# Attention's weighted sums transposed onto the two column halves of the array, two query tiles a step, gates from the unnormalised sums

## The chip, the cores and the metric

One Trainium2 chip, one of its cores. The metric is the device time of one execution in microseconds (us), the median of several runs. Lower is better.

## What is computed

Three blocks follow each other: attention over a band of keys and a few global ones, a layer of eight experts with one expert for each token, and a gated product.

```python
# attention: batch 2, 8 heads, 768 positions, head dimension 64; 8 global keys, 96 local ones
scores = q @ k.T / 8 + bias          # bias: -slope[head] * distance
scores = where(keep, scores, -1e9)   # keep: key among the first 8, or 0 <= query - key < 96
a = exp(scores - max(scores)); a = a / (sum(a) + 1e-9)
x = a @ v                            # gathered to (1536 tokens, 512)

# experts: 8 of them, 512 -> 1024 -> 512
logits = x @ w_gate; e = argmax(logits)
gate = softmax(logits)[e]; eom = sigmoid(x @ w_output_gate)[e]
y = gate * eom * (relu(x @ w1[e]) @ w2[e])

# gated product, width 1536
out = ((y @ w_a) * (y @ w_b)) @ w_out
```

## The kernel before

The kernel runs the blocks one after the other; the change is in attention and its names reach a little into the routing that follows.

**Attention** goes over 48 units (batch, pair of heads, query tile of 128). For one unit, 256 key columns are laid out side by side: 96 keys of the tile ahead, 32 global columns, the tile's own 128 (the first tile of a head has its own 128 alone). A unit has three parts, written for different units in one turn of the loop, so that the engines overlap: in turn n the loop writes `score` of unit n, `trans` of unit n-2 and `av` of unit n-3.

- `score`: the two heads of a pair sit in the two halves of the partitions (64 rows each), so their matmuls use the two row halves of TensorE's array. VectorE adds the bias and takes the row's extreme in one instruction (L489), ScalarE takes the exponential (L493).
- `trans`: the weights `pe` (queries in the partitions) are transposed by TensorE in chunks of 128 keys (L505), and copied out of PSUM as `pt` (keys in the partitions), two times in three by ScalarE (L509), else by VectorE (L511).
- `av`: `pt` is the stationary operand and the values `vc`, 64 columns and a 65th of ones, the moving one (L523, L526). The result `ps_a` has queries in the partitions, and its 65th column is the sum of the weights. Every second unit VectorE adds 1e-9 (L530), takes the reciprocal (L531) and multiplies into `x` (L535).

**Gates.** `gate` transposes a finished piece of `x` back (L548, `ps_xt`), ScalarE copies it as `xT` (L550), and TensorE multiplies it by the two gates' 16 columns (L555, `ps_g`); VectorE adds the four pairs of heads up in `lg` (L558, L560). A queue `gq` holds these steps, one a turn.

**Routing** sorts tokens by expert. `r_expert` finds each token's expert, `r_rank` its place (a few small matmuls into `ps_r`), `r_hot` and `r_ids` make the list of tokens. For the first batch these come from a queue `eq`, one entry a turn of the attention loop; for the second they follow the loop. `eload` and `esplit` fetch and split the first expert's weights in the last turns: a cast on ScalarE (L103) and a subtraction on GpSimd (L104).

All float32 products of attention are two matmul instructions each in the trace (transposes one). The order on each engine is the order of the code; engines meet by semaphores. PSUM holds two score buffers, two for `trans` (shared with `ps_xt`), one for `ps_a` and one for `ps_g`.

Of the kernel before, what the change touches and what calls it, by code (L numbers as in the profile page):

```python
# [46 lines left out]
def moe_block_kernel(ctx, tc, qd, kd, vd, kt, vn, nv, wg, we, wm, out):  # L47
# [19 lines left out]
    wg_sb = con([P, 4, 16], "wg_sb")  # L67
    lg = con([P, NT, 16], "lg")
# [324 lines left out]
    with ExitStack() as att:  # L393
# [33 lines left out]
        nc.sync.dma_start(wg_sb, wg)  # L427
        make_identity(nc, ident)
# [39 lines left out]
        units = [(b, p, i) for b in range(B) for p in range(4) for i in range(QT)]  # L468
        PE_, PT, pA = {}, {}, {}
# [4 lines left out]
        def score(u):  # L474
            b, p, i = u
            k0, n, b0 = geom(i)

            ps = psS.tile([P, 2, 512], F32, tag="s", name="ps_s")
            bp = b * 4 + p
            ko, qo = (0, 0) if bp or i < 2 else (K1, Q0)  # L480
            for j in range(2):
                r = slice(j * D, (j + 1) * D)
                T.matmul(ps[:, j, 0:n], QQ[bp, qo][r, i * P - qo:(i + 1) * P - qo], KC[bp, ko][r, k0 - ko:k0 - ko + n],
                         start=True, stop=True)
            pe = wrk.tile([P, 2, 256], F32, tag="pe", bufs=4, name="pe")
            mx = wrk.tile([P, 2], F32, tag="mx", bufs=6, name="mx")

            for j in range(2):
                V.tensor_tensor_reduce(  # L489
                    out=pe[:, j, 0:n], in0=ps[:, j, 0:n], in1=bias[2 * p + j][:, b0:b0 + n], op0=ALU.add, op1=ALU.min,  # L490
                    scale=-0.125, scalar=3e38, accum_out=mx[:, j:j + 1])
            for j in range(2):
                A.activation(pe[:, j, 0:n], pe[:, j, 0:n], AF.Exp, bias=mx[:, j:j + 1], scale=-1.0)  # L493
            PE_[u] = pe

        ncopy = [0]

        def trans(u):
            b, p, i = u
            pe = PE_.pop(u)  # L500
            nch = 1 if i == 0 else 2
            ps = psT.tile([P, 2, 2, P], F32, tag="t", name="ps_t")
            for j in range(2):
                for c in range(nch):
                    T.transpose(ps[:, j, c, :], pe[:, j, c * P:(c + 1) * P], ident)  # L505
            pt = wrk.tile([P, 2, 2, P], F32, tag="pt", name="pt")
            ncopy[0] += 1
            if ncopy[0] % 3 or u in units[-2:]:
                A.copy(pt[:, :, 0:nch, :], ps[:, :, 0:nch, :])  # L509
            else:  # L510
                V.tensor_copy(pt[:, :, 0:nch, :], ps[:, :, 0:nch, :])  # L511
            PT[u] = pt

        def av(u):
            b, p, i = u
            pt = PT.pop(u)
            if i % 2 == 0:
                pA[b, p] = psA.tile([P, 2, 2, 65], F32, tag="a", name="ps_a")
            pa = pA[b, p]
            for j in range(2):  # L520
                bh = b * H + 2 * p + j
                if i == 0:
                    T.matmul(pa[:, 0, j, :], pt[:, j, 0, :], VC[bh][:, 0, :], start=True, stop=True)  # L523
                else:
                    for c in range(2):
                        T.matmul(pa[:, i % 2, j, :], pt[:, j, c, :], VC[bh][:, 2 * i - 1 + c, :], start=(c == 0), stop=(c == 1))  # L526
            if i % 2 == 1:
                pa = pA.pop((b, p))
                rs = wrk.tile([P, 2, 2, 1], F32, tag="rs", bufs=4, name="rs")
                V.tensor_scalar(rs, pa[:, :, :, 64:65], 1e-9, None, ALU.add)  # L530
                V.reciprocal(rs, rs)  # L531
                m = b * 3 + i // 2
                if p == 0:
                    xt[m] = xp.tile([P, 2, DM], F32, tag="x", name=f"x{m}")
                V.tensor_tensor(  # L535
                    xt[m][:, :, 2 * p * D:(2 * p + 2) * D].rearrange("p i (j d) -> p i j d", j=2),
                    pa[:, :, :, 0:64], rs.to_broadcast([P, 2, 2, 64]), ALU.mult)
                if p == 3:
                    nc.sync.dma_start(x_dram[m * 256:(m + 1) * 256, 0:DM].rearrange("(i p) d -> p i d", p=P), xt[m])


        xTs = {}

        def gate(m, p, k):
            if k == 0:
                pt = psT.tile([P, 2, P], F32, tag="t", bufs=2, name="ps_xt")
                for j in range(2):
                    T.transpose(pt[:, j, :], xt[m][:, j, p * P:(p + 1) * P], ident)  # L548
                xTs[m, p] = wrk.tile([P, 2, P], F32, tag="xT", bufs=3, name="xT")
                A.copy(xTs[m, p], pt)  # L550
            else:
                xs = xTs.pop((m, p))
                pg = psG.tile([P, 2, 16], F32, tag="g", bufs=1, name="ps_g")
                for j in range(2):
                    T.matmul(pg[:, j, :], xs[:, j, :], wg_sb[:, p, :], start=True, stop=True)  # L555
                L = lg[:, 2 * m:2 * m + 2, :]
                if p == 0:
                    V.tensor_copy(L, pg)  # L558
                else:
                    V.tensor_tensor(L, pg, L, ALU.add)  # L560
# [4 lines left out]
        gq, eq = [], []  # L565
# [20 lines left out]
        for n in range(nu + 3):  # L586
            if n < nu:
                b, p, i = units[n]
                nxt = b * 4 + p + 1
                if i in (2, 3) and nxt + 1 < 8:  # L590
                    (loadq if i % 2 else loadk)(nxt + 1)
                if i in (4, 5) and nxt < 8:
                    loadv(2 * nxt + i - 4)
                if b == 0 and p < 3 and i in (3, 5):
                    make_bias(2 * p + 2 + (i - 3) // 2)
                score(units[n])
            if 0 <= n - 2 < nu:
                trans(units[n - 2])
            if 0 <= n - 3 < nu:
                av(units[n - 3])  # L600
            for q in (gq, eq):
                if q:
                    q.pop(0)()
            if 0 <= n - 3 < nu:
                b, p, i = units[n - 3]
                if i % 2 == 1:
                    m = b * 3 + i // 2
                    gq += [lambda k=k, m=m, p=p: gate(m, p, k) for k in range(2)]
                if n == 29:
                    route(0, 6)  # L610
                    factor(0, 6)
            for _ in range(2 if n >= 7 else 0):
                if cl:
                    cl.pop(0)()
            if n == 3:
                flags()
# [577 lines left out]
```

## Time and profile before

| | |
|---|---|
| median of 3 runs | 657.28 us (655.16 to 664.75) |
| the profiled execution | 651.98 us |
| its span, first to last instruction | 650.3 us |
| PE busy | 602.3 us, 93% |
| DVE / ACT / POOL busy | 401.7 / 310.2 / 215.7 us |
| granted clock of PE, mean | 0.971 |
| attention | from 4.5 us (first score matmul) to some 124 us (last gates) |

The span's share of an engine is an average over blocks of very different kind; attention is read in its own stretch. PE is TensorE's matmuls, PEld its weight loads, DVE VectorE, ACT ScalarE, POOL GpSimd. A matmul's end is modelled, and its shown duration reaches over the next one; where blocks of matmuls follow each other, the distance from start to start tells what a block takes.

### The profile page before, as it was taken

How to read it: one execution, taken by the hardware profiler on the slowest of the kernel's cores; microseconds unless marked ns; L12 is line 12 of the kernel's file. 1: busy time of each engine (PE TensorE's matmuls, PEld its weight loads, DVE VectorE, ACT ScalarE, POOL GpSimd, SP SyncE). 2: the span in 40 equal slices, each digit the busy share in tenths (PEclk: the TensorE clock that was granted, in tenths of full speed). 3: DMA queues.
4: the chain of work that ended last, by engine and by line, in shares of the span. 5: the costliest groups of instructions: out<-in, count | busy, mean ns of one | idle time of the engine just before them, and what ended most of it. 6: DMA issues, size and time to landing. Idle time of an engine off the chain costs nothing. (4 is left out here: it accounts for less than half of the span.)

```text
span 650.3 us, 9929 instructions
## 1 busy us (share of the span) xinstructions
PE 602.3 (93%) x3503; PEld 517.7 (80%) x3503; DVE 401.7 (62%) x936; ACT 310.2 (48%) x609; POOL 215.7 (33%) x167
## 2 busy tenths in 40 slices
PE   6999999667999999799788999999999999999995
PEld 4778778557999988689787888888888888888884
DVE  6566776559684798799996765754551675131312
ACT  3655557324554666577664656554521554111110
POOL 3000004135343655465354543363330354001012
PEclk9999999858999999799899999999999999999998
DMA  7454541435747777777635332232110130001011
GB/s 259 136 159 147 185 162 44 110 123 196 255 144 251 212 242 257 232 234 243 200 129 175 103 119 71 65 130 65 66 65 1 65 130 0 1 1 65 1 66 65
DMA packets 33357, 84.09 MB, mean 129 GB/s; under 512 B 5232, under 2 KB 11632, under 8 KB 33296
## 3 DMA queue, kind: packets, MB, share of 16 engines
q1 hardware_dynamic: 21200, 53.29, 25.9%
q10 hardware_dynamic: 9936, 23.14, 10.6%
q0 software_dynamic: 2160, 6.91, 2.9%
q8 instruction: 30, 0.49, 0.3%
q14 instruction: 31, 0.25, 0.1%
HBM read 72.23 MB, written 11.10 MB: 128 GB/s over the span
## 5 line engine op out<-in xcount | busy, mean ns | idle before, releaser
L104 POOL TENSOR_TENSOR wl<-st,wh 128x1024 fp32r<-128x1024 f32 x27 | 65.8, 2441 | 173.8 <-ACT wh L103 162.9
L1097 PE MATMUL ps_ab<-yTh,wh 128*128 128x512 f32 x288 | 112.7, 391 | 1.9 <-ACTq L996 1.9
L1098 PE MATMUL ps_ab<-yTl,wh 128*128 128x512 f32 x288 | 112.7, 391 | 0.0
L1099 PE MATMUL ps_ab<-yTh,wl 128*128 128x512 f32 x288 | 112.4, 390 | 0.0
L880 POOL TENSOR_TENSOR wl<-wl,st 128x512 fp32r<-128x512 f32 x36 | 56.4, 1568 | 141.7 <-ACT wl L879 132.3
L1106 DVE TENSOR_TENSOR a<-a,ps_ab 128x512 f32<-128x512 f32 x36 | 24.7, 686 | 112.5 <-PE ps_ab L1099 106.9
L103 ACT CAST wh<-st 128x1024 fp32r<-128x1024 f32 x64 | 67.2, 1052 | 13.4 <-DMA st<-we 12.0
L700 PE MATMUL ps_y<-h,wl 128*128 128x256 f32 (+5 forms) x256 | 70.5, 275 | 0.0
L700 PE MATMUL ps_h<-x,wl 128*128 128x256 f32 (+5 forms) x256 | 69.3, 271 | 0.0
L1097 PEld LDWEIGHTS ps_ab<-yTh,wh 128*128 128x128 f32 x288 | 54.0, 188 | 14.1 <-ACTq L996 2.1
L1104 ACT COPY a<-ps_ab 128x512 f32<-128x512 f32 x36 | 21.1, 585 | 90.8 <-PE ps_ab L1099 89.0
L493 ACT ACTIVATE pe<-pe,mx 128x256 f32<-128x256 f32 (+1 forms) x96 | 41.8, 483 | 47.4 <-DVE mx L489 47.1
L1099 PEld LDWEIGHTS ps_ab<-yTh,wl 128*128 128x128 f32 x288 | 54.0, 188 | 11.9
L1098 PEld LDWEIGHTS ps_ab<-yTl,wh 128*128 128x128 f32 x288 | 54.0, 188 | 11.7
L696 PE MATMUL ps_y<-h,wh 128*128 128x448 f32 (+3 forms) x160 | 54.3, 393 | 7.7 <-DVE h L714 7.1
L104 DVE TENSOR_TENSOR wl<-st,wh 128x1024 fp32r<-128x1024 f32 x37 | 52.4, 1419 | 10.2 <-ACT wh L103 10.2
L1107 ACT CAST gh<-a 128x512 fp32r<-128x512 f32 x36 | 22.3, 619 | 71.7 <-DVE a L1106 71.4
L1120 PE MATMUL ps_o<-wl,gh 128*128 128x512 f32 x144 | 56.3, 391 | 0.0
L1119 PE MATMUL ps_o<-wh,gh 128*128 128x512 f32 x144 | 56.2, 390 | 0.0
L1121 PE MATMUL ps_o<-wh,gl 128*128 128x512 f32 x144 | 56.2, 390 | 0.0
L881 POOL TENSOR_TENSOR wl<-wl,td 128x512 fp32r<-128x512 f32 x36 | 52.5, 1459 | 2.8
L700 PEld LDWEIGHTS ps_y<-h,wl 128*128 128x128 f32 x256 | 50.8, 198 | 0.0
(181 smaller groups left out, 1286.2 us busy)
## 6 DMA issues: line engine op xcount, KB each, us to landing
st<-we SPq DMA_DIRECT2D x63, 512.0 KB, 4.1
st<-wm ACTq DMA_DIRECT2D x36, 512.0 KB, 3.8
vc<-vd SPq DMA_DIRECT2D x16, 357.5 KB
k<-kd SPq DMA_DIRECT2D x7, 464.0 KB, 4.9
x_dram<-x SPq DMA_DIRECT2D x6, 512.0 KB, 2.9
st<-y_dram SPq DMA_DIRECT2D x6, 512.0 KB
q<-qd SPq DMA_DIRECT2D x7, 384.0 KB, 5.3
y_dram<-zero SPq DMA_DIRECT2D x4, 256.0 KB
```

The costliest lines, as they stand in the source:

```text
L103: A.copy(wh, st)
L104: eng.tensor_tensor(wl, st, wh[:, :].bitcast(F32), ALU.subtract)
L696: T.matmul(pt[:, 0:2 * n].rearrange("p (s n) -> p s n", s=2), a, M[:, k], start=(k == 0), stop=False)
L700: T.matmul(pt[:, 0:n], b, M[:, k, 0], start=False, stop=(k == last))
L880: G.tensor_tensor(wl_, wl_.bitcast(F32), sv[:, :, 0].bitcast(F32), ALU.add)
L881: G.tensor_tensor(wl_, wl_.bitcast(F32), td[:, :].bitcast(F32), ALU.mult)
L1097: T.matmul(pt, wh[:, s_, k, :], yh[:, k, :], start=(k == 0), stop=False)
L1098: T.matmul(pt, wh[:, s_, k, :], yl[:, k, :], start=False, stop=False)
L1099: T.matmul(pt, wl_[:, s_, k, :], yh[:, k, :], start=False, stop=(k == 3))
L1119: T.matmul(PO[c][t_], a, wh, start=(f == FG * g), stop=False)
L1120: T.matmul(PO[c][t_], a, wl_, start=False, stop=False)
L1121: T.matmul(PO[c][t_], l, wh, start=False, stop=(f == FG * g + FG - 1))
```

## The change

A step now holds two query tiles: 24 units (batch, pair of heads, pair of tiles), with `trans` one step behind `score`, `av` two and a new `rows` three. The weighted sum is transposed: `vc` (64 columns, no ones) is the stationary operand, `pt` the moving one of 128 columns, and the head of a pair decides which half of the partitions of `ps_a`, so which half of the array's columns, its result takes. So `ps_a` has the head's dimension in the partitions, not normalised. ScalarE copies it as `xT`. From `xT`, `rows` makes both results: the gates, by a table `wg2` in which each head of a pair has its own 16 columns, and, by a transpose, the rows of `x`; both are divided by the sum on VectorE. The sum of the weights comes from the exponential's own accumulator (`accum_out=sm`) in place of the column of ones. The four pairs' gates are kept apart in `lgp` and added up once, with the last pair. The order of entries in `eq`, the weight loads and the other fillers is thinned to the 24 steps: two entries of `eq` a step.

```diff
-            VC[bh] = raw.tile([P, 2 * QT - 1, 65], F32, tag="vc", bufs=4, name=f"vc{bh}")
+            VC[bh] = raw.tile([P, 2 * QT - 1, D], F32, tag="vc", bufs=4, name=f"vc{bh}")
...
-        units = [(b, p, i) for b in range(B) for p in range(4) for i in range(QT)]
+        units = [(b, p, m) for b in range(B) for p in range(4) for m in range(QT // 2)]
...
         def score(u):
-            ps = psS.tile([P, 2, 512], F32, tag="s", name="ps_s")
-            for j in range(2):
-                T.matmul(ps[:, j, 0:n], QQ..., KC..., start=True, stop=True)
+            ps = psS.tile([P, 2, 2, 256], F32, tag="s", name="ps_s")
+            for t_ in range(2):
+                for j in range(2):
+                    T.matmul(ps[:, j, t_, 0:n], QQ..., KC..., start=True, stop=True)
...
-                A.activation(pe[:, j, 0:n], pe[:, j, 0:n], AF.Exp, bias=mx[:, j:j + 1], scale=-1.0)
+                    A.activation(pe[:, t_, j, 0:n], pe[:, t_, j, 0:n], AF.Exp, bias=mx[:, t_, j:j + 1], scale=-1.0,
+                                 accum_out=sm[:, t_, j:j + 1])
...
         def trans(u):
+                if t_:
+                    A.copy(pt, ps)
+                else:
+                    V.tensor_copy(pt[:, :, 0:nch, :], ps[:, :, 0:nch, :])
...
         def av(u):
-            for j in range(2):
-                    for c in range(2):
-                        T.matmul(pa[:, i % 2, j, :], pt[:, j, c, :], VC[bh][:, 2 * i - 1 + c, :], start=(c == 0), stop=(c == 1))
+                for c in range(nch):
+                    for j in range(2):
+                        T.matmul(pa[j * D:(j + 1) * D, t_, :], VC[b * H + 2 * p + j][:, max(2 * i - 1, 0) + c, :], pt[:, j, c, :],
+                                 start=(c == 0), stop=(c == nch - 1))
+            XT_[u] = wrk.tile([P, 2, P], F32, tag="xT", bufs=2, name="xT")
+            A.copy(XT_[u], pa)
+
+        def rows(u):
+            px = psG.tile([P, 2, P + 32], F32, tag="g", name="ps_x")
+            for t_ in range(2):
+                T.matmul(px[:, t_, P:P + 32], xT[:, t_, :], wg2_sb[:, p, :], start=True, stop=True)
+            for t_ in range(2):
+                T.transpose(px[:, t_, 0:P], xT[:, t_, :], ident)
+            V.tensor_scalar(rs, rs, 1e-9, None, ALU.add)
+            V.reciprocal(rs, rs)
+            V.tensor_tensor(lgp[...], px[:, :, P:P + 32]..., rs.to_broadcast([P, 2, 2, 16]), ALU.mult)
+            if p == 3:
+                V.tensor_reduce(lg[:, 2 * m:2 * m + 2, :], lgp[...], axis=AX.X, op=ALU.add)
+            V.tensor_tensor(xt[m][...], px[:, :, 0:P]..., rs.to_broadcast([P, 2, 2, D]), ALU.mult)
...
-            if 0 <= n - 2 < nu:
-                trans(units[n - 2])
-            if 0 <= n - 3 < nu:
-                av(units[n - 3])
-            for q in (gq, eq):
-                if q:
-                    q.pop(0)()
+            if 0 <= n - 1 < nu:
+                trans(units[n - 1])
+            if 0 <= n - 2 < nu:
+                av(units[n - 2])
+            if 0 <= n - 3 < nu:
+                rows(units[n - 3])
+            for _ in range(2):
+                if eq:
+                    eq.pop(0)()
...
         run(r_expert(6, 10, lg))
-        while gq:
-            gq.pop(0)()
```

TensorE, two turns in the middle of the loop before: one with a gate's matmuls (`ps_g`), one with its transposes (`ps_xt`).

```order
L483 MATMUL ps_s<-k_747,q_777 128x256 x2
L505 MATMUL ps_t<-ident,pe 128x128 x4
L526 MATMUL ps_a<-vc_973,pt 128x65 x2
L526 MATMUL ps_a<-vc_1004,pt 128x65 x2
L555 MATMUL ps_g<-wg_sb,xT 128x16 x2
L483 MATMUL ps_s<-k_747,q_777 128x256 x2
L505 MATMUL ps_t<-ident,pe 128x128 x4
L526 MATMUL ps_a<-vc_973,pt 128x65 x2
L526 MATMUL ps_a<-vc_1004,pt 128x65 x2
L548 MATMUL ps_xt<-ident,x_998 128x128 x2
```

One step of the loop now, here one in which `av` is that of a head's first pair of tiles (its first tile has one chunk of keys, so six matmuls stand for eight).

```order
L494 MATMUL ps_s<-k_368,q_370 128x256 x4
L520 MATMUL ps_t<-ident,pe 128x128 x8
L537 MATMUL ps_a<-pt,vc_595 64x128
L537 MATMUL ps_a<-pt,vc_597 64x128
L537 MATMUL ps_a<-pt,vc_595 64x128
L537 MATMUL ps_a<-pt,vc_597 64x128
L537 MATMUL ps_a<-pt,vc_595 64x128
L537 MATMUL ps_a<-pt,vc_597 64x128
L547 MATMUL ps_x<-wg_sb,xT 128x32 x2
L549 MATMUL ps_x<-ident,xT 128x128 x2
```

The kinds of work stand together for two tiles, the two heads' products alternate in `av`, and `vc` and `pt` have changed places; the number of products is the same.

VectorE, where the first batch is routed, before: between `r_expert` (L208 to L221) and the first instruction of `r_rank` (L259) stands the work of a turn.

```order
L217 TENSOR_TENSOR OHb<-r_t,r_111 128x48
L219 TENSOR_SCALAR r_e<-r_111 128x6
L221 TENSOR_SCALAR r_e<-r_e 128x6
L489 ISA pe,mx<-ps_s,bias_194 128x256
L489 ISA mx 128x1
L489 ISA pe,mx<-ps_s,bias_195 128x256
L489 ISA mx 128x1
L511 COPY pt<-ps_t 128x512
L259 TENSOR_TENSOR r_t<-ps_r,OHb 128x48
```

The same place now (`r_expert` is L210 to L223, `r_rank` begins with L261).

```order
L555 TENSOR_TENSOR lgp<-ps_x,sm 128x2x32
L563 TENSOR_TENSOR x_1020<-ps_x,sm 128x2x128
L210 TENSOR_REDUCE r_112<-lg 128x6
L212 TENSOR_TENSOR ex<-lg,r_112 128x48
L215 SCALAR_TENSOR_TENSOR r_t<-ex,i_100 128x48
L217 TENSOR_REDUCE r_112<-r_t 128x6
L219 TENSOR_TENSOR OHb<-r_t,r_112 128x48
L221 TENSOR_SCALAR r_e<-r_112 128x6
L223 TENSOR_SCALAR r_e<-r_e 128x6
L261 TENSOR_TENSOR r_t<-ps_r,OHb 128x48
```

The two entries of the queue now follow each other in one step; TensorE's matmuls into `ps_r`, which read `OHb`, stand behind that step's transposes and ahead of the next step's scores.

VectorE behind the loop, before: the last gates' sum (L560, second row of it) comes behind `r_expert` of the tokens ahead of it.

```order
L560 TENSOR_TENSOR lg<-ps_g,lg 128x32
L208 TENSOR_REDUCE r_111<-lg 128x4
L210 TENSOR_TENSOR ex<-lg,r_111 128x32
L213 SCALAR_TENSOR_TENSOR r_t<-ex,i_99 128x32
L215 TENSOR_REDUCE r_111<-r_t 128x4
L217 TENSOR_TENSOR OHb<-r_t,r_111 128x32
L219 TENSOR_SCALAR r_e<-r_111 128x4
L221 TENSOR_SCALAR r_e<-r_e 128x4
L560 TENSOR_TENSOR lg<-ps_g,lg 128x32
L245 TENSOR_REDUCE ne<-OHb 128x8
```

The same place now.

```order
L555 TENSOR_TENSOR lgp<-ps_x,sm 128x2x32
L559 TENSOR_REDUCE lg<-lgp 128x32
L563 TENSOR_TENSOR x_1155<-ps_x,sm 128x2x128
L210 TENSOR_REDUCE r_112<-lg 128x4
L212 TENSOR_TENSOR ex<-lg,r_112 128x32
L215 SCALAR_TENSOR_TENSOR r_t<-ex,i_100 128x32
L217 TENSOR_REDUCE r_112<-r_t 128x4
L219 TENSOR_TENSOR OHb<-r_t,r_112 128x32
L221 TENSOR_SCALAR r_e<-r_112 128x4
L223 TENSOR_SCALAR r_e<-r_e 128x4
L247 TENSOR_REDUCE ne<-OHb 128x8
```

The last `rows`, with its gates' sum and its piece of `x`, has moved ahead of `r_expert` of the earlier tokens.

## Rows read from the trace of the kernel before

**Rows 1.** Windows: length, busy of PE, PEld, DVE, ACT, POOL; granted clock; DMA share, GB/s.

```profile
60.00:80.00 20.00, 19.39 (x162) 16.08 (x163) 13.29 (x65) 10.26 (x27) 0.00 (x0) 1.00 0.57 189
80.00:100.00 20.00, 18.51 (x152) 14.88 (x152) 14.69 (x68) 11.10 (x29) 0.00 (x0) 1.00 0.46 153
120.00:140.00 20.00, 10.01 (x62) 8.60 (x61) 10.22 (x59) 3.31 (x11) 3.76 (x4) 0.61 0.45 128
```

**Rows 2.** PE's waits in 12 to 122 us: in total, times, longest (us).

```profile
PE ps_t L505 <- ACT pt L509: 3.1, 10, 0.6
```

**Rows 3.** Timeline of PE: start, length (us), what, instructions merged.

```profile
42.54 0.70 PE L483 MATMUL ps_s<-k,q 64*128 64x256 f32 x4
43.17 0.66 PE L505 MATMUL ps_t<-ident,pe 128*128 128x128 f32 x4
43.66 1.00 PE L526 MATMUL ps_a<-vc,pt 128*128 128x65 f32 x8
44.50 0.39 PE L548 MATMUL ps_xt<-ident,x 128*128 128x128 f32 x2
44.82 0.49 PE L483 MATMUL ps_s<-k,q 64*128 64x128 f32 x4
...
46.78 0.57 PE L555 MATMUL ps_g<-wg_sb,xT 128*128 128x16 f32 x4
47.28 0.70 PE L483 MATMUL ps_s<-k,q 64*128 64x256 f32 x4
```

**Rows 4.** Timeline of PE where unit 4 and unit 46 begin.

```profile
12.15 0.70 PE L483 MATMUL ps_s<-k,q 64*128 64x256 f32 x4
...
110.80 0.70 PE L483 MATMUL ps_s<-k,q 64*128 64x256 f32 x4
```

**Rows 5.** Timeline of PE from 47.2 to 47.6 us alone.

```profile
47.28 0.49 PE L483 MATMUL ps_s<-k,q 64*128 64x256 f32 x2
```

**Rows 6.** Groups of PE in 12 to 122 us: busy us, mean ns of one.

```profile
L526 PE MATMUL ps_a<-vc,pt 128*128 128x65 f32 x320 | 40.3, 269 | 0.1
...
L483 PE MATMUL ps_s<-k,q 64*128 64x256 f32 x148 | 26.0, 428 | 0.0
...
L483 PE MATMUL ps_s<-k,q 64*128 64x128 f32 x28 | 3.4, 323 | 0.0
```

**Rows 7.** Groups of ACT and DVE in 12 to 122 us.

```profile
L493 ACT ACTIVATE pe<-pe,mx 128x256 f32<-128x256 f32 x75 | 34.1, 501 | 39.8 <-DVE mx L489 39.8
...
L489 DVE CUSTOM_DVE_ANT_0 pe<-ps_s,bias 128x256 f32<-128x256 f32 x74 | 28.4, 421 | 14.5 <-PE ps_s L483 10.2 <-ACT pt L509 3.9 <-ACT pe L493 0.3
...
L509 ACT COPY pt<-ps_t 128x512 f32<-128x512 f32 x25 | 14.1, 566 | 1.6 <-PE ps_t L505 1.6
...
L511 DVE COPY pt<-ps_t 128x512 f32<-128x512 f32 x15 | 10.3, 688 | 0.6 <-PE ps_t L505 0.3
L535 DVE TENSOR_TENSOR x<-ps_a,rs 128x256 f32<-128x256 f32 x24 | 10.2, 424 | 0.8
...
L550 ACT COPY xT<-ps_xt 128x256 f32<-128x256 f32 x23 | 8.5, 370 | 1.7 <-PE ps_xt L548 1.6
...
L531 DVE RECIPROCAL rs<-rs 128x4 f32<-128x4 f32 x24 | 4.3, 178 | 0.8
...
L230 ACT ACTIVATE r_sz<-r_sz 128x6 f32<-128x6 f32 x1 | 0.2, 208 | 1.4 <-DVE r_sz L229 1.4
```

**Rows 8.** Timeline of PE near the start.

```profile
10.71 1.11 PE L505 MATMUL ps_t<-ident,pe 128*128 128x128 f32 x4
```

**Rows 9.** Timeline of DVE behind the loop.

```profile
121.97 0.19 DVE L208 TENSOR_REDUCE r<-lg 128x4 f32<-128x32 f32 x1
...
123.17 0.17 DVE L221 TENSOR_SCALAR r_e<-r_e 128x4 f32<-128x4 f32 x1
...
123.68 0.28 DVE L245 TENSOR_REDUCE ne<-OHb 128x8 f32<-128x80 bf16 x1
...
129.04 0.26 DVE L296 TENSOR_TENSOR ids_i<-ps_i,ids_f 128x96 int32<-128x96 f32 x1 [0.28 <-PE ps_i L294]
```

More of the change, by code (lines that the diff above doesn't have):

```diff
@@ L486, in score @@
-            mx = wrk.tile([P, 2], F32, tag="mx", bufs=6, name="mx")
-            for j in range(2):
[L489 to L492, printed above, removed]
-                A.activation(pe[:, j, 0:n], pe[:, j, 0:n], AF.Exp, bias=mx[:, j:j + 1], scale=-1.0)
-            PE_[u] = pe
-        ncopy = [0]
+            b, p, m = u
@@ new lines, in score @@
+            for t_ in range(2):
+                k0, n, b0 = geom(2 * m + t_)
+                for j in range(2):
+                    V.tensor_tensor_reduce(
+                        out=pe[:, t_, j, 0:n], in0=ps[:, j, t_, 0:n], in1=bias[2 * p + j][:, b0:b0 + n], op0=ALU.add, op1=ALU.min,
+                        scale=-0.125, scalar=3e38, accum_out=mx[:, t_, j:j + 1])
+                for j in range(2):
+                    A.activation(pe[:, t_, j, 0:n], pe[:, t_, j, 0:n], AF.Exp, bias=mx[:, t_, j:j + 1], scale=-1.0,
+                                 accum_out=sm[:, t_, j:j + 1])
@@ L542, in moe_block_kernel @@
[L542 to L560, printed above, removed]
+            PT[u] = []
@@ new lines, in trans @@
+            for t_ in range(2):
+                nch = chunks(2 * m + t_)
+                ps = psT.tile([P, 2, 2, P], F32, tag="t", name="ps_t")
+                for j in range(2):
+                    for c in range(nch):
+                        T.transpose(ps[:, j, c, :], pe[:, t_, j, c * P:(c + 1) * P], ident)
+                pt = wrk.tile([P, 2, 2, P], F32, tag="pt", bufs=4, name="pt")
+                if t_:
+                    A.copy(pt, ps)
+                else:
+                    V.tensor_copy(pt[:, :, 0:nch, :], ps[:, :, 0:nch, :])
+                PT[u].append(pt)
@@ new lines, in av @@
+        def av(u):
+            b, p, m = u
+            pa = psA.tile([P, 2, P], F32, tag="a", name="ps_a")
+            for t_, pt in enumerate(PT.pop(u)):
+                i = 2 * m + t_
+                nch = chunks(i)
+                for c in range(nch):
+                    for j in range(2):
+                        T.matmul(pa[j * D:(j + 1) * D, t_, :], VC[b * H + 2 * p + j][:, max(2 * i - 1, 0) + c, :], pt[:, j, c, :],
+                                 start=(c == 0), stop=(c == nch - 1))
+            XT_[u] = wrk.tile([P, 2, P], F32, tag="xT", bufs=2, name="xT")
+            A.copy(XT_[u], pa)
@@ L587, in moe_block_kernel @@
             if n < nu:
-                b, p, i = units[n]
+                b, p, m = units[n]
                 nxt = b * 4 + p + 1
[L590 to L595, printed above, removed]
+                if m == 1 and nxt + 1 < 8:
+                    loadk(nxt + 1)
+                    loadq(nxt + 1)
@@ L604, in moe_block_kernel @@
-            if 0 <= n - 3 < nu:
[L605 to L612, printed above, removed]
+                rows(units[n - 3])
+            for _ in range(2):
+                if eq:
+                    eq.pop(0)()
+            if n == 14:
+                route(0, 6)
+                factor(0, 6)
@@ L640, in moe_block_kernel @@
         r_ids(oh, 12, psS, "s", 2)
-        pd = psS.tile([P, 2, 256], F32, tag="s", name="ps_d")
+        pd = psS.tile([P, 2, 2, 256], F32, tag="s", name="ps_d")
         for _ in range(10):
-            T.matmul(pd[:, 0, 0:P], ident, ident, start=True, stop=True)
+            T.matmul(pd[:, 0, 0, 0:P], ident, ident, start=True, stop=True)
     pse = ExitStack()
```

116 lines of the change are left out of this document (58 added, 58 removed).

## The prediction

> **What bounds the kernel now.** I read the windows first, since a share over the whole span mixes blocks. In attention TensorE is the full engine: 19.39 of 20 us busy between 60 and 80 us and 18.51 between 80 and 100, where the first batch is routed, while VectorE has 13.29 and 14.69 and ScalarE 10 to 11 [rows 1]. Its clock is granted in full there (1.00, the level of 2.4 GHz). Then the waits: over the whole of attention TensorE's matmuls waited only 3.1 us for ScalarE's copies of `pt` [rows 2]. So attention takes what TensorE's blocks take, and the change must be costed block by block. What follows attention (routing's tail, experts, the gated product) keeps its instructions and starts from the token list, so I let it shift as a whole.
>
> **The blocks before.** From start to start in the timeline [rows 3]: a unit's scores take 0.63 us (42.54 to 43.17), its four transposes 0.49, its eight `av` matmuls 0.84, then either two transposes of `x` 0.32 or four gate matmuls 0.50 (46.78 to 47.28). A unit with transposes is 2.28 us, one with gates 2.46, so two tiles take 4.74. Between the starts of unit 4 and unit 46 lie 98.65 us for 42 units, 14.09 for a pair of heads [rows 4].
>
> Two facts of these rows carry the estimate. First, the two heads' score matmuls, in the two row halves of the array, run at the same time: in a cut of 0.4 us two of them cover 0.49 us together [rows 5], while one alone lasts 0.43 on the mean [rows 6]. Second, 128 more columns lengthen a matmul by 428 - 323 = 105 ns [rows 6]; I take 0.11 us for each 128 columns that stream. A score block of 0.63 is then two pairs of 256 columns (0.42) and 0.21 of change-over: a half's weights loaded with nothing to cover them and the array changed between halves and whole.
>
> **The blocks after, for two full tiles.**
> - Scores: the same eight matmuls with one change-over instead of two: 0.63 + 2 x 0.21 = 1.05 (before 1.26).
> - Transposes: the same eight: 0.49 + 4 x 0.11 = 0.93 (before 0.98).
> - `av`: the same sixteen instructions, but each streams 128 columns instead of 65, over 64 stationary columns instead of 128. If the two column halves run in pairs as the row halves do, eight slots of 0.11 and a change-over of 0.21 make 1.09 (before 1.68). If they do not, sixteen slots and the change-over make 1.97. No row shows column halves; these are the bounds, and I take the pair, because it is nearest to the row of the row halves [rows 5] and the code writes the heads alternately, as the scores are written.
> - `rows`: four gate instructions and two transposes, the count of before: 0.50 + 2 x 0.11 = 0.72 (before 0.82).
>
> The sum is 3.79 us a step in pairs and 4.67 unpaired, against 4.74. In the step of a head's first tile, half the scores have 128 columns (-0.21), two transposes (-0.22) and four `av` instructions (-0.22, unpaired -0.44) are missing: 3.14 or 3.80. A pair of heads is 10.72 or 13.14. Over the 21 steps that answer to units 4 to 46 this is 75.0 or 92.0 us against 98.65: **23.6 us** gained, or 6.7.
>
> **What takes some of it back.**
> - *Other engines in a plain step.* By whole durations [rows 7], ScalarE has four exponentials (2.00), a `pt` copy (0.57) and the copy of `xT` (0.37): 2.94. VectorE has four bias instructions (1.68), a `pt` copy (0.69), three small ones (at most 0.18 each) and the product into `x` (0.42): 3.33. Both lie below 3.79 and may overlap, since TensorE needs in a step what they made in the step ahead. They cost nothing there; VectorE's cover is only 0.46 us.
> - *The accumulator of the exponential.* No row of ScalarE has one. Nothing at the low end, a small instruction more (0.208 [rows 7]) at the other; VectorE's own accumulator is read in 83 ns. At 0.21 ScalarE has 3.78, still hidden; I take nothing, and the upper end goes into a rival.
> - *Routing of the first batch.* `r_expert` and `r_rank` now stand in one step. TensorE reaches the matmuls into `ps_r` when its step's transposes are done; VectorE still has the two products (0.18 + 0.42) and then `r_expert`, 1.37 us (121.97 to 123.17 and the last 0.17 [rows 9]). TensorE stands idle some 2.3 us with handover, once, and the next scores are queued behind. Before, a turn's work lay between. The bounds are 0 and 3; I take 2.3.
> - *Crowded steps.* In three steps two entries of `r_hot` join VectorE (about 1.2 us of work on top of 3.33) and in four a cast of 1.05 us joins ScalarE. By durations 0.2 to 0.7 us over TensorE's step each; durations overlap on these engines, so I take 2 us in all, bounds 0 and 6.
> - *The tail.* Before, from unit 46's scores to the sum over tokens (L245) 12.88 us [rows 4, 9]. After, a whole step (3.79), one without scores (2.74), `av` and `rows` (1.81), the last `rows` (0.72), some 0.3 of handover, and on VectorE the gates, their sum, the piece of `x` and `r_expert`, now behind it, 2.2: 11.56. A gain of 1.3, unpaired a loss of 1.3.
> - *The start.* The first eight transposes run at the other level of the clock (1.11 us for four [rows 8] where four later take 0.66), before and after alike. The second step can start no earlier than the same loads; I take nothing, bound a gain of 1.
>
> The sum in pairs is 23.6 - 2.3 - 2.0 + 1.3 = **20.6 us**. The profiled execution, 651.98 us, becomes 631.4; it lies 5.3 below the median of the runs shown (657.28), which spread over 9.6. On the median's scale I forecast **637 us**.
>
> **Rivals.**
> 1. *The column halves do not run together.* Then the change does not do what it says. Against it stand the scores [rows 5], for it that the two heads read the same partitions here, and there different ones. 6.7 - 4.3 - 1.3 = 1.1 us: 656 us. 15 in 100.
> 2. *ScalarE and VectorE become the bound.* For it: VectorE's 3.33 is close to 3.79, and ScalarE gains four accumulators. Against: the plain sums above. If an exponential costs 0.4 more, ScalarE has 4.54 a step, 0.97 over the mean step of 3.57; over 24 steps that takes 23 us, so 659 us. 9 in 100. The Trainium skill, "TensorEngine Tiling (Array Packing)", section PSUM Bottleneck, says that tiling speeds up TensorE but not the emptying of PSUM, which may then bind. This case's rows say how near that is: by them 0.46 us of VectorE's step is left, and by the rule alone the time would be this rival's.
> 3. *Slower: the clock falls in attention.* The place is the steady loop. In the stretch 120 to 140, where TensorE was half idle behind routing, the granted clock was 0.61 on the mean; at the lower level (1.2 GHz) four transposes took 1.11 instead of 0.66 [rows 1, 8]. If the new loop left TensorE waiting in every step so that the lower level held, the blocks would double: a pair of heads 21.4 us instead of 14.1, over seven pairs 51 us lost, 708 us. From some 67 us of attention at the lower level on the kernel is over 2% slower (each such us costs about half of itself, and 20.6 + 13 must be lost). Against: TensorE stays the fullest engine by the sums, and its one long stand is 2.3 us. 4 in 100.
>
> **How the numbers follow.** 72 in 100 for the forecast in pairs, where the bounds of the charges give 630 to 643. The range: the low end is all charges hidden and the start gained (23.6 + 1.3 + 1 = 26, 631), with 2 us of scatter between runs: 629. At the upper end it takes in the unpaired case, 656. Above it lie most of rival 2 and rival 3, together some 12 in 100, and a few in 100 below. A measurement of this kernel tells about 2% (13 us) from no change. Faster by more than that: the forecast and a part of rivals in between, 74 in 100. Within it: rivals 1 and 2, 20. Slower: rival 3 and rival 2 with an accumulator that costs over 0.5, 6.
>
> **What would show it.** In the profile after, `av`'s matmuls of two heads should start within some 10 ns of each other and eight of them (four products) take about 0.5 us; where they follow each other at 0.11 us, rival 1 holds. A full step should last about 3.8 us from scores to scores, with no wait of TensorE for `pt` or `xT`. A ScalarE step over 3.6 us and TensorE waiting for `pe`, `pt` or `xT` speak for rival 2; a granted clock under 1.00 between 15 and 95 us for rival 3. One wait of about 2 us for `OHb` should stand where the first batch is routed, and L247 should come some 21 us earlier than 123.68. The forecast is wrong from its base if the experts' stage does not shift with the token list (129.04 [rows 9]), because its loads of weights come no earlier.

## The result and the profile after

The changed kernel takes 637.74 us (median of 4 runs, 636.68 to 638.83) against 660.84 (4 runs, 655.16 to 664.75) for the one before on the same chip: ratio 0.9657, 95% interval [0.9568, 0.9746]. The profiled execution took 637.93 us, its span is 636.2. The kernel before ran in groups of times on these chips (near 654, 664 and 674 us), so its medians move with the group; the two traces, 651.98 against 637.93, differ by 14.1 us, and it is these 14.1 us that the text below accounts for.

Windows of the kernel after (length, busy of PE, PEld, DVE, ACT, POOL; granted clock; DMA share, GB/s):

```profile
20.00:40.00 20.00, 20.00 (x201) 15.47 (x201) 16.51 (x77) 15.64 (x59) 0.00 (x0) 1.00 0.59 183
40.00:60.00 20.00, 20.00 (x193) 15.13 (x193) 15.67 (x70) 14.57 (x52) 0.00 (x0) 1.00 0.52 174
60.00:80.00 20.00, 18.05 (x168) 13.99 (x169) 16.17 (x82) 12.18 (x42) 0.59 (x1) 0.91 0.62 212
80.00:100.00 20.00, 18.68 (x170) 14.11 (x166) 18.08 (x71) 16.08 (x54) 8.86 (x4) 0.91 0.20 64
```

From 20 to 60 us TensorE shows no gap at all. From 60 us on it has gaps, VectorE is fuller than before (16.17 and 18.08 against 13.29 and 14.69 [rows 1]), and the granted clock is no longer 1.00.

Two steps of the steady loop in the timeline of PE after (start, length, what, instructions):

```profile
44.13 1.13 PE L494 MATMUL ps_s<-k,q 64*128 64x256 f32 x8
45.20 1.09 PE L520 MATMUL ps_t<-ident,pe 128*128 128x128 f32 x8
46.22 0.88 PE L537 MATMUL ps_a<-pt,vc 128*64 128x128 f32 x12
47.03 0.63 PE L547 MATMUL ps_x<-wg_sb,xT 128*128 128x32 f32 x4
47.49 0.41 PE L549 MATMUL ps_x<-ident,xT 128*128 128x128 f32 x2
47.84 0.93 PE L494 MATMUL ps_s<-k,q 64*128 64x128 f32 x8
48.70 1.09 PE L520 MATMUL ps_t<-ident,pe 128*128 128x128 f32 x8
49.72 1.09 PE L537 MATMUL ps_a<-pt,vc 128*64 128x128 f32 x16
50.74 0.63 PE L547 MATMUL ps_x<-wg_sb,xT 128*128 128x32 f32 x4
```

Read from start to start: scores 1.07 us (44.13 to 45.20), eight transposes 1.02, sixteen weighted sums 1.02 (49.72 to 50.74), rows and gates 0.81; a step is 3.71 (44.13 to 47.84), each step with one of its blocks reduced by a head's first tile. In a cut of 0.1 us two sums of two heads cover 0.33 together; they start 7 ns apart, and pairs follow at 0.109 us:

```profile
49.72 0.33 PE L537 MATMUL ps_a<-pt,vc 128*64 128x128 f32 x2
```

Waits of PE after, from 12 to 108 us (us in total, times, longest):

```profile
PE ps_r L259 <- DVE r_e L221: 1.9, 1, 1.9
PE ps_x L547 <- DVE sm L551: 1.7, 2, 1.4
...
PE ps_i L296 <- DVE x L563: 1.3, 1, 1.3
...
PE ps_t L520 <- ACT pt L523: 0.2, 1, 0.2
```

The 3.1 us for `pt` [rows 2] are down to 0.2. What is new is waiting for VectorE, once for `r_expert`, once for `ps_i` behind the product into `x`, and in the tail for the single buffer of `ps_x`.

The first of these places in the timeline of PE after:

```profile
62.34 0.41 PE L549 MATMUL ps_x<-ident,xT 128*128 128x128 f32 x2
64.71 0.18 PE L259 MATMUL ps_r<-OHb,ltri 128*128 128x48 bf16 x1 [1.95 <-DVE r_e L221]
64.73 0.27 PE L259 MATMUL ps_r<-OHb,onesb 128*128 128x40 bf16 x5
64.93 1.31 PE L494 MATMUL ps_s<-k,q 64*128 64x256 f32 x8
66.17 1.54 PE L520 MATMUL ps_t<-ident,pe 128*128 128x128 f32 x6
67.64 1.82 PE L537 MATMUL ps_a<-pt,vc 128*64 128x128 f32 x16
69.39 0.63 PE L547 MATMUL ps_x<-wg_sb,xT 128*128 128x32 f32 x4
```

The wait makes this step 5.96 us. The next takes 5.27 with no wait: its blocks are longer (1.24, 1.47 and 1.75 from start to start), at a granted clock of 0.50 from 66 to 68 us, which is the lower level.

VectorE and, below it, POOL near 80 us after (rows of two timelines):

```profile
80.95 0.86 DVE L551 TENSOR_SCALAR sm<-sm 128x4 f32<-128x4 f32 x1
81.84 0.18 DVE L552 RECIPROCAL sm<-sm 128x4 f32<-128x4 f32 x1
...
83.82 2.09 DVE L248 CAST OHs<-ne 128x8 bf16<-128x8 f32 x1
```

```profile
79.41 2.37 POOL L106 TENSOR_TENSOR wl<-st,wh 128x1024 fp32r<-128x1024 f32 x1 [64.44 <-ACT wh L105]
83.53 2.35 POOL L106 TENSOR_TENSOR wl<-st,wh 128x1024 fp32r<-128x1024 f32 x1 [1.75 <-ACT wh L105]
```

An add on four numbers a partition takes 0.86 us, a cast of eight 2.09, where 0.16 and 0.17 are usual; they end at 81.81 and 85.91, when POOL's subtractions end (81.78, 85.88). Two more adds take 1.16 and 0.96 under the two later subtractions; the steps around those two stay at 3.72 and 3.70, so a held add need not cost a step anything.

The end of attention on VectorE after:

```profile
105.09 0.22 DVE L555 TENSOR_TENSOR lgp<-ps_x,sm 128x64 f32<-128x64 f32 x1 [0.75 <-PE ps_x L549]
105.35 0.58 DVE L559 TENSOR_REDUCE lg<-lgp 128x32 f32<-128x256 f32 x1
...
107.66 0.23 DVE L555 TENSOR_TENSOR lgp<-ps_x,sm 128x64 f32<-128x64 f32 x1 [1.12 <-PE ps_x L549]
...
110.02 0.28 DVE L247 TENSOR_REDUCE ne<-OHb 128x8 f32<-128x80 bf16 x1
...
115.39 0.26 DVE L298 TENSOR_TENSOR ids_i<-ps_i,ids_f 128x96 int32<-128x96 f32 x1 [0.28 <-PE ps_i L296]
```

L247 comes 13.7 us earlier than its counterpart [rows 9], `ids_i` 13.66. From there to the end of the span it is 520.8 us (636.2 less 115.39), before 521.3: what follows shifted as a whole, as assumed.

**Where the 13.66 us come from.** The scores of units 4 and 5, the third step, start at 11.22 instead of 12.15 [rows 4]: 0.93. The 21 steps from there to the last scores (95.79) take 84.57 instead of 98.65: 14.08. From the last scores to `ids_i` it is 19.59 instead of 18.24: -1.35. Of the 84.57, 21 x 3.71 = 77.9 are steady steps; four steps are longer, 5.96, 5.27, 5.64 and 5.10, together 7.1 too much, and the two after the start are 0.5 shorter together.

### The profile page after: what moved, and what is told of

Its sections match the earlier page's. It is cut to its first block, busy times and chain, and to the rows that moved or that the text cites. A ratio compares the mean times of both kernels' runs of the same rounds, so it can differ in the third digit from the quotient of the medians.

```text
span 636.2 us, 10043 instructions
## 1 busy us (share of the span) xinstructions
PE 589.5 (93%) x3503; PEld 503.1 (79%) x3503; DVE 407.3 (64%) x951; ACT 314.2 (49%) x696; POOL 215.8 (34%) x167
## 5 line engine op out<-in xcount | busy, mean ns | idle before, releaser
L700 PE MATMUL ps_y<-h,wh 128*128 128x448 f32 (+3 forms) x160 | 56.3, 405 | 5.6 <-DVE h L718 5.1
L504 ACT ACTIVATE pe<-pe,mx 128x256 f32<-128x256 f32 (+1 forms) x96 | 45.9, 479 | 29.3 <-DVE mx L500 29.3
```

The costliest lines, as they stand in the source:

```text
L700: T.matmul(pt[:, 0:2 * n].rearrange("p (s n) -> p s n", s=2), a, M[:, k], start=(k == 0), stop=False)
```

## The experiments

All edits are against the changed kernel (637.74 us; 636.65 when measured again, number 10). A ratio, where one is given, is to the kernel before. Steps are read from scores to scores in TensorE's timeline.

**1. Do the heads run together because they are written alternately?**

```diff
-                for c in range(nch):
-                    for j in range(2):
+                for j in range(2):
+                    for c in range(nch):
                         T.matmul(pa[j * D:(j + 1) * D, t_, :], VC[b * H + 2 * p + j][:, max(2 * i - 1, 0) + c, :], pt[:, j, c, :],
```

> In av all chunks of one head come before those of the other, instead of the two heads alternating. Theory: the column halves run together because consecutive products go to different halves; then the block of sixteen instructions, 1.02 us in the changed kernel, becomes some 1.9 us, a step 4.55 instead of 3.71, and the kernel 17 to 20 us longer: about 656 us. Rival: the array finds the pairs by itself across four instructions; then the block stays at 1.02 us and the time at 638.

638.93 us (638.52 to 639.62), ratio 0.976 [0.971, 0.9811]. In the timeline of PE:

```profile
50.05 1.15 PE L537 MATMUL ps_a<-pt,vc 128*64 128x128 f32 x16
51.12 0.63 PE L547 MATMUL ps_x<-wg_sb,xT 128*128 128x32 f32 x4
```

1.07 us for the sixteen instead of 1.02, a step 3.76. With each head's two products (four instructions) in a row, the other half's product still starts beside them. Alternation is worth 0.05 us a step; my theory on it was wrong, the rival right.

**2. The half picked by the tile instead of the head.**

```diff
-                for c in range(nch):
-                    for j in range(2):
-                        T.matmul(pa[j * D:(j + 1) * D, t_, :], VC[b * H + 2 * p + j][:, max(2 * i - 1, 0) + c, :], pt[:, j, c, :],
+                for j in range(2):
+                    for c in range(nch):
+                        T.matmul(pa[t_ * D:(t_ + 1) * D, j, :], VC[b * H + 2 * p + j][:, max(2 * i - 1, 0) + c, :], pt[:, j, c, :],
```

> Both heads of a tile go to the same half of the columns (the tile picks the half instead of the head), so the sums land in other places and the output is another one; number, shape and order of the instructions stay. Theory: the gain of av is that the halves run together; now sixteen slots of 0.11 us follow each other, 1.9 us a block, and the time is about 656 us. Rival: the gain is that only 64 columns are loaded for each product; then the block stays at 1.0 us and the time at 638.

647.75 us (646.37 to 649.32), ratio 0.989 [0.9835, 0.9945]. Steps of 4.20, 4.19 and 3.93, halfway:

```profile
45.45 1.58 PE L537 MATMUL ps_a<-pt,vc 128*64 128x128 f32 x16
46.96 0.63 PE L547 MATMUL ps_x<-wg_sb,xT 128*128 128x32 f32 x4
```

The order did change, against what the expectation says: the heads come in turn, as in number 1, which by itself costs 0.05 us. 1.51 us for sixteen. The first four follow at 0.11 us, then the second tile's products, which sit in the other half, start beside the first tile's remaining four; its own last four stand alone again. The edit did not part what it was to part, hence number 3.

**3. All sums in one half**, so that nothing can pair.

```diff
-                for c in range(nch):
-                    for j in range(2):
-                        T.matmul(pa[j * D:(j + 1) * D, t_, :], VC[b * H + 2 * p + j][:, max(2 * i - 1, 0) + c, :], pt[:, j, c, :],
+                for j in range(2):
+                    for c in range(nch):
+                        T.matmul(pa[0:D, t_, j, :], VC[b * H + 2 * p + j][:, max(2 * i - 1, 0) + c, :], pt[:, j, c, :],
...
-            A.copy(XT_[u], pa)
+            A.copy(XT_[u][0:D], pa[0:D, :, 0, :])
```

> The change with all weighted sums of both heads and both tiles in the lower half of the array's columns, one head after the other, with the second head's block left out of the rows (that half of the transposed block is zero throughout). Nothing can pair now, neither across heads nor across tiles. If pairing is the gain, the sums of a step go back to 16 products at about 0.109 us each, 1.7 to 1.9 us in place of 1.02, and full steps to 4.4 to 4.6 us; over 21 steps that is 15 to 19 us, so the time is 652 to 657. The rival: most of the gain over the kernel before comes from the 65th column and the second pass of gates that were dropped, and the halves matter little: steps below 4.1 us, 646 or less.

654.78 us (654.0 to 657.79). Steps of 4.57, 4.58 and 4.35:

```profile
49.02 1.96 PE L540 MATMUL ps_a<-pt,vc 128*64 128x128 f32 x16
50.91 0.63 PE L550 MATMUL ps_x<-wg_sb,xT 128*128 128x32 f32 x4
```

1.89 us for sixteen at 0.109 each. Three steps are 13.50 instead of 11.13, 2.37 more; over 21 steps 16.6 us, and the profiled execution (654.0) is 16.1 us longer than the changed kernel's. The products still load 64 columns each, so it is not the narrower operand that makes the block short. Without pairing nothing is left of the gain (654.0 against 651.98 before), as the prediction had it; number 4 tells what the change is worth without the transposed form.

**4. Steps of two tiles alone**, with the sums, the ones column and the gates of the kernel before.

```diff
-            pa = psA.tile([P, 2, P], F32, tag="a", name="ps_a")
+            pa = psA.tile([P, 2, 2, 65], F32, tag="a", name="ps_a")
...
-                for c in range(nch):
-                    for j in range(2):
-                        T.matmul(pa[j * D:(j + 1) * D, t_, :], VC[b * H + 2 * p + j][:, max(2 * i - 1, 0) + c, :], pt[:, j, c, :],
+                for j in range(2):
+                    for c in range(nch):
+                        T.matmul(pa[:, t_, j, :], pt[:, j, c, :], VC[b * H + 2 * p + j][:, max(2 * i - 1, 0) + c, :],
```

> Two query tiles a step as in the changed kernel, but the weighted sums, the column of ones and the gates from the normalised rows as before. Theory: the steps alone save one change-over of the array for two tiles (0.2 to 0.3 us a step) and the waits for copies, so a pair of heads takes some 12.6 us against 14.1 before and 11.1 in the changed kernel: 645 to 650 us. Rivals: all of the gain is from the steps (638), or none (657 to 660).

649.12 us (10 runs, 645.79 to 652.12), ratio 0.9938 [0.9908, 0.9968], so within 2% of the kernel before.

```profile
47.89 1.13 PE L492 MATMUL ps_s<-k,q 64*128 64x256 f32 x8
...
51.93 0.93 PE L492 MATMUL ps_s<-k,q 64*128 64x128 f32 x8
...
56.22 1.13 PE L492 MATMUL ps_s<-k,q 64*128 64x256 f32 x8
```

Steps of 4.27, 4.28 and 4.04, 12.59 a pair of heads against 14.09 [rows 4]: this part alone is worth 1.50 per pair of heads, 10.5 us over 21 steps, and the transposed sums another 1.46. Its steps of 6.22, 5.69 and 4.81 us, while the first batch is routed, give 4.4 of that back. The profiled execution, the fastest of the ten, is 645.79: of the 14.1 us between the two traces, 6.2 come with the steps of two tiles alone and 7.9 with the transposed sums in pairs (11.4 by the medians, 649.12 and 637.74). Without pairing the transposed form (13.50) would be worse than this.

**5. Routing one step ahead of its use.**

```diff
+            if n == 14:
+                route(0, 6)
+                factor(0, 6)
-            for _ in range(2):
+            for _ in range(1 if n < 16 else 2):
                 if eq:
                     eq.pop(0)()
```

> The first batch's r_expert is taken a step ahead of r_rank, one entry of the queue in each of these two steps. Theory: TensorE no longer stands 2 us before the matmuls into ps_r, and the blocks behind, which ran at the lower level of the clock, run at the full one: 2.25 and 1.56 us less, 634 us, with a granted clock of 1.00 between 60 and 75 us. Rival: the wait moves to the next step, since VectorE has the same work: 638. A third: the wait goes but the clock falls all the same: 635.5.

636.6 us (635.47 to 640.04), ratio 0.9738 [0.967, 0.9806]. PE's waits:

```profile
PE ps_r L259 <- DVE x L563: 1.9, 1, 1.9
...
PE ps_i L296 <- DVE x L563: 1.3, 1, 1.3
```

The operands were there, but `ps_r` shares one buffer with `ps_x` and now waits until VectorE has read that: the same 1.9 us under another name, the step still 5.85. The rival (the wait moves) was right. Yet the next step took 3.71 instead of 5.27: the clock did not fall (granted 1.00 from 58 to 96 us).

**6. The add of 1e-9 left out**, to see what POOL holds up.

```diff
-            V.tensor_scalar(rs, rs, 1e-9, None, ALU.add)
```

> The change with the 1e-9 left out of the sums' reciprocals (the add at L551, in place, SBUF to SBUF); a sum of exponentials with its maximum taken out is at least 1, so nothing else changes. It asks what VectorE waited for when three of these adds took 0.86 to 1.16 us in place of 0.16 while GpSimd worked on the second half of the attention. My theory: it is the kind of instruction that is held, a one-input arithmetic operation that reads and writes SBUF alone, for as long as GpSimd's own operation lasts; the reciprocal behind it was never held, so the hold goes with the add, the steps of 5.64 and 5.10 us come down to 4.5 or less, the cast at L248 still takes some 2 us, and the time is 634 to 636. The rival: whatever VectorE does first on SBUF alone is held, so the reciprocal takes 0.8 to 1.2 us in the same places, the steps stay, and the time is 637 to 639.

635.41 us (632.54 to 638.77). The reciprocal is now first, and under POOL's subtraction (81.26 to 83.63) it is as short as ever:

```profile
82.73 0.17 DVE L551 RECIPROCAL sm<-sm 128x4 f32<-128x4 f32 x1
```

None of the four is held; three of them stand well inside a subtraction, one begins 0.05 us before its end. The step of 5.64 is 4.79, the one of 5.10 is 3.71. So it is the kind of instruction that is held, not whatever comes first; my theory. It missed in two numbers: a step at 4.79 and not below 4.5, and the cast at L248, which no longer met a subtraction and was short. In this trace, that of the slowest of the four runs, the step behind the routing's wait took 6.51 us, more than the 5.27 of the changed kernel, at the lower level of the clock for longer:

```profile
66.00:68.00 2.00, 2.00 (x10) 1.18 (x9) 0.81 (x5) 0.00 (x0) 0.00 (x0) 0.50 0.85 340
68.00:70.00 2.00, 2.00 (x14) 1.67 (x14) 1.76 (x10) 1.66 (x7) 0.00 (x0) 0.50 0.06 23
```

**7. No accumulator in the exponential.**

```diff
-                    A.activation(pe[:, t_, j, 0:n], pe[:, t_, j, 0:n], AF.Exp, bias=mx[:, t_, j:j + 1], scale=-1.0,
-                                 accum_out=sm[:, t_, j:j + 1])
-            PE_[u], SM[u] = pe, sm
+                    A.activation(pe[:, t_, j, 0:n], pe[:, t_, j, 0:n], AF.Exp, bias=mx[:, t_, j:j + 1], scale=-1.0)
+            PE_[u], SM[u] = pe, one4
```

> The change without the sums from ScalarE: the exponentials go without the accumulator, and a tile of ones stands for the sums, so the rows and gates are not divided. It takes 88 reads of 0.187 us away from ScalarE, 16.5 us in all. My theory is the prediction's zero for them: ScalarE ended nothing in the steady steps (15.6 us busy of 20), so full steps stay at 3.71 us, the tail loses a few tenths, and the time is 637 to 638. The rival: the reads sit between the exponentials and the transposes that wait for them, so steps come down by a tenth or two, 635 or less.

Undivided gates route the tokens otherwise, and all that follows becomes another computation: 1075.84 us says nothing. Attention lies ahead of that and can be read: steps are 3.71 as with the accumulator, the last scores to `ids_i` 19.35, between the 19.59 and 19.22 of the two traces of the changed kernel. Hidden in the loop, and in the tail no more than those two differ. The reads cost ScalarE itself less than they last: exponentials of 128x256 follow at 0.49 us with them and at 0.40 without.

**8. Routing's sums beside `ps_a` in its bank.**

```diff
-            pa = psA.tile([P, 2, P], F32, tag="a", name="ps_a")
+            pa = bank[:, 0:2 * P].rearrange("p (t q) -> p t q", t=2)
...
-            eq.extend([lambda: run(r_expert(a, b, lg)), lambda: run(r_rank(a, b, psG, "g", 1))])
+            eq.extend([lambda: run(r_expert(a, b, lg)), lambda: run(r_rank(a, b, PR, "g", 1))])
...
-            eq.extend([lambda: r_ids(oh, b, psG, "g", 1), lambda: r_sum(b)])
+            eq.extend([lambda: r_ids(oh, b, PR, "g", 1), lambda: r_sum(b)])
```

> The change with the routing's two sums (ps_r and ps_i in the attention) in the unused half of the bank of ps_a, not in the single buffer that they share with ps_x. If the shared buffer is what holds them, TensorE waits only for what they are computed from: the step of 5.64 us comes down to about 4, the one of 5.96 us stays (there it waited for r_expert's own chain on VectorE), and the time is 635 to 637. The rival: the buffer was free at those moments and the operands late; both steps stay, and the time is 638.

633.52 us (632.62 to 636.58). The step of 5.64 came down to 5.12 only: in one tile with `ps_a` the sum `ps_i` waits 1.0 us for the copy of `xT`.

```profile
PE ps_a L259 <- DVE r_e L221: 2.0, 1, 2.0
...
PE ps_a L296 <- ACT xT L541: 1.0, 1, 1.0
```

Inconclusive on the buffer. The 3 us came from elsewhere: after the same wait of 2.0 us for `r_e` the next step took 3.71, and so did the one behind 5.12, with the granted clock at 1.00 and no cast held.

**9. Two buffers more in the tail.**

```diff
-            px = psG.tile([P, 2, P + 32], F32, tag="g", name="ps_x")
+            px = (psS if u in units[-2:] else psG).tile([P, 2, P + 32], F32, tag="s" if u in units[-2:] else "g", name="ps_x")
```

> The change with the last two ps_x in the pool of ps_s alone. If the single buffer is what made the end of the attention 1.3 us longer than before in place of 1.3 us shorter, TensorE runs its last rows ahead and the stretch from the last score to ids_i falls from 19.6 us to 18 or less; time 636. The rival: it is VectorE's own work in these rows (reciprocal, gates, the sum over heads of 0.59 us, the x product, some 1.75 us a step) that sets the pace; the stretch stays above 19 us and the time is 637 to 638.

636.87 us (635.38 to 638.17), ratio 0.9698 [0.9589, 0.9807]. From the last scores to `ids_i` 18.72 us, between the two expectations (19.59 and 19.22 in two traces of the changed kernel). The last rows follow at 1.57 instead of 2.57 us on VectorE:

```profile
103.22 0.23 DVE L555 TENSOR_TENSOR lgp<-ps_x,sm 128x64 f32<-128x64 f32 x1 [0.37 <-PE ps_x L549]
...
104.79 0.23 DVE L555 TENSOR_TENSOR lgp<-ps_x,sm 128x64 f32<-128x64 f32 x1
```

The single buffer is worth 0.5 to 0.9 us; most of the rest is VectorE's own work there. The time is no shorter than that of number 10, so this gain shows in the trace alone.

**10. The changed kernel again**, for a second trace.

> The changed kernel once more, as the measure for the other two on the same chip, and for a second trace of it: is the lower clock that followed the routing's wait in the first trace (blocks of 1.3 to 2.1 us in place of 1.0 in two stretches) a fixed cost of that wait, or does it come and go? If fixed, the step after the one of 5.96 us again takes about 5.3 us and the granted clock from 60 to 80 us is 0.91; if it comes and goes, that step takes 3.7 us with the same wait ahead of it, and the span to ids_i is 1.5 to 3 us shorter. The time is 636 to 639 either way.

636.65 us (6 runs, 635.3 to 643.27), ratio 0.9706 [0.9613, 0.9799]. Steps of 5.96, 5.28, 5.47 and 5.31: the lower clock came again in the same places. By "fixed" it should then follow such a wait in every kernel; it did not in numbers 3, 5, 8 and 9. Number 9 has the same wait on the same operand, but two stretches of the changed kernel and of number 9 read:

```profile
64.00:66.00 2.00, 1.29 (x14) 0.92 (x14) 1.50 (x10) 0.00 (x0) 0.00 (x0) 0.94 0.99 348
66.00:68.00 2.00, 2.00 (x12) 1.50 (x12) 1.70 (x10) 1.15 (x5) 0.00 (x0) 0.50 0.48 194
```

```profile
64.00:66.00 2.00, 1.20 (x14) 0.92 (x14) 1.51 (x9) 0.00 (x0) 0.00 (x0) 1.00 1.05 392
66.00:68.00 2.00, 2.00 (x25) 1.58 (x23) 1.85 (x10) 1.22 (x5) 0.00 (x0) 1.00 0.55 222
```

So neither answer holds as put: two traces of one program agree, and it is not a fixed price of the wait.

**11. The mends together**: number 5, number 6, number 9, and routing's sums in the pool of `ps_t`.

```diff
-            eq.extend([lambda: run(r_expert(a, b, lg)), lambda: run(r_rank(a, b, psG, "g", 1))])
+            eq.extend([lambda: run(r_expert(a, b, lg)), lambda: run(r_rank(a, b, psT, "t", 2))])
...
-            V.tensor_scalar(rs, rs, 1e-9, None, ALU.add)
...
+            for _ in range(1 if n < 16 else 2):
```

> The change with four mends together: the routing begins a step earlier than it is needed and gives one piece a step at first; its two sums go to the pool of ps_t, not the single buffer of ps_x; the add of 1e-9 is left out; and the last two ps_x go to the pool of ps_s, so that three rows of sums no longer pass one buffer at the end. My theory of where the prediction's missing microseconds went (a wait for VectorE's routing chain behind one buffer, the held add, the low clock after them, and rows in single file at the end) says that the four steps over 5 us in the attention come down to below 4.2 us, ids_i comes at 107 to 109 us in place of 115.4, and the time is 629 to 632. The rival: VectorE, 78 to 90% busy there, is the true limit of that stretch, so the excess moves to other steps: ids_i at 111 or later and 633 or more.

630.59 us (6 runs, 629.03 to 633.77) beside 636.65 for the changed kernel (number 10); ratio to the kernel before 0.9601 [0.9523, 0.9678]. `ids_i` comes at 108.14 instead of 114.87. The four long steps are 4.91, 3.71, 3.96 and 3.71; the first missed the 4.2, since `ps_r` still waits 0.90 us for VectorE:

```profile
63.98 0.18 PE L259 MATMUL ps_r<-OHb,ltri 128*128 128x48 bf16 x1 [0.90 <-DVE sm L551]
```

Of the 6.73 us the wait at the routing gave 1.05, the step after it 1.57, the next two 1.51 and 1.60, the tail 1.51, and the start took back 0.5. Where number 6, without the add alone, had 4.79, this kernel has 3.96: 0.8 us for the other pool and the thinner queue together. All its runs lie below all of the changed kernel, by about 1% in the median.

## Why the prediction came out right, and where it did not

**The mechanism held.** TensorE's blocks set attention, and the column halves run in pairs as the row halves do [rows 5]: 7 ns apart, eight slots of 0.109 us (0.11 taken), sixteen products in 1.02 us (1.09 predicted), 1.89 when forced into one half (1.97 predicted). Numbers 1 to 3, which change where the products land or in what order, show it. Rival 1 is out. Its price for the block was right; that number 3 gave 654.78 where 656 stood is in part the luck of the base (below), since its sum puts the profiled execution at 650.9 and that took 654.0.

**Steady steps: forecast 2.9 us too short.** Predicted 75.0 for 21 steps, 77.9 at 3.71. The full blocks sum to 3.92 instead of 3.79: the transposes measured 1.02 where I had 0.93, the rows 0.81 where I had 0.72. I had kept a change-over for scores and sums alone; eight transposes at 0.109 are 0.87, so the transposes carry some 0.15 of it too.

**Routing and crowded steps: 7.1 instead of 4.3.** The stall was well sized (2.3 predicted, 2.25 measured in the step). The "crowded steps" (2, bounds 0 to 6) are where the sum failed: 4.9 us. Two things were not in it. One is the add on `sm`, SBUF to SBUF where L530 read PSUM, which VectorE could not run while POOL subtracts; `x` came late and `ps_i` stood behind it (number 6 took 0.85 off that step). The other is the lower clock after a stand of TensorE: 1.56 us in the step after the routing's, 2.80 in number 6 (3.71 in numbers 5, 8 and 9, with such a wait but the clock at 1.00). In the step of 5.10 the lower clock and the held cast lie over each other: with the clock at 1.00 that step took 3.70 and 3.71 (numbers 5 and 9), but the two behind it some 4.5 and 3.97, where the transposes waited, mostly for VectorE: with the clock at 1.00 the held cast and add cost 1.05 there. How the changed kernel's 1.39 us divide was not parted. Rival 3's sign came (a granted clock of 0.91 from 60 to 100 us), but not its time: it had the lower level in the whole loop, and the clock fell in two short stretches behind the waits.

**The tail: a loss of 1.35 instead of a gain of 1.3.** I counted TensorE's blocks and 2.2 us of VectorE once, behind them. In fact, as the trace shows, three rows follow each other through the one buffer of `ps_x`, 2.2 to 2.6 us apart; the sum over heads is 0.58 us each, and I had put it into the 2.2. Number 9 took off 0.5 to 0.9 by buffers, number 11 1.5 to 1.9 with the add gone as well.

**The accumulator**: 0.187 us a read, 96 reads, close to the upper end of 0.21, though the exponentials come only 0.09 further apart, and nothing of it in a steady step (number 7). Rival 2 is out for the plain loop: TensorE is busy 20.00 of 20. Its time was summed 1 us too low (657.28 - 20.6 + 23 is 660).

**The start**: 0.93, the bound named (1) and not taken; what gave it was not asked.

**The base.** By my own sum the profiled execution should have become 631.4; it became 637.93, 6.5 us more. That the forecast of 637 nonetheless met the median is owed to the step by which I added 5.3 us for the median of before: the changed kernel's four runs lie within 2.2 us of each other around its profiled one (of six later ones one stood out, 643.27), so there was nothing to add. Two errors, of 6.5 and 5.3 us, cancelled.

**Still open**: what decides whether the clock falls after a wait of 2 us. In seven traces it fell (twice the changed kernel, numbers 1, 2, 4, 6 and 7), in four it did not (3, 5, 8, 9), with waits of 1.7 to 2.0 us at the same place of the program and TensorE full ahead of them. Number 11 waited 0.9 us there and kept its clock. So what part of a mend's gain is the clock, and would come again in another program, is not shown.

## What to carry to other kernels

Matmuls with 64 output partitions that land in different column halves ran two at a time here, even when each half's instructions came four in a row; placed in one half they took 1.89 us instead of 1.02, and the transposed form was then not worth its wider stream. When TensorE's loop is made faster, cost the side jobs (routing, tails) again on VectorE by its order and its single buffers, since a pair of operations that used to have another turn between them now meets TensorE. And subtract a profiled execution from a profiled execution: a scatter that the kernel before shows need not carry over.

## What the runs showed of the hardware

VectorE's add and cast from SBUF to SBUF stood until a subtraction of POOL (2.36 us) ended: 0.86 to 1.16 us and 2.09 (2.27 in numbers 1, 5, 9 and 10) instead of 0.16 and 0.17, while a reciprocal (0.17, number 6), copies from PSUM and the bias instructions ran beside it. The Trainium skill, "SBUF — State Buffer", section "Who interferes with whom", states that copies, casts and tensor_scalar can enter a mode that uses both of VectorE's ports, and that this mode and GpSimd exclude each other for a whole instruction; the rows agree, down to the reciprocal, which that list does not have.

The array paired products of the two column halves across an order of two products and two (number 1, 1.07 us for sixteen) and paired the tail of one tile with the head of the next (number 2, 1.51).
